# A delta-rule attention with a routed MoE behind it: first expert in parts of 320 and 160 tokens, down tiles in different PSUM tensors, VectorE's substitution in the third pair

## Chip, core and metric

One core of one Trainium2 chip. The metric is the time of one execution in device microseconds.

## What is computed

Attention with a state per head (4 batches, 8 heads, 768 tokens, head size 48), then a mixture of 8 experts (384 to 1024 to 384) on its output. The router is sticky: a token takes its own best expert or that of the token before it.

```python
for t in range(S):                      # per batch and head, state is 48 x 48
    y[t] = q[t] @ state
    state += beta[t] * outer(k_n[t], v[t] - state.T @ k_n[t])
logits = x @ w_gate;  keep = sigmoid(x @ w_local) >= 0.5
e = prev_e if keep and prev_e >= 0 else argmax(logits)
out[t] = softmax(logits)[e] * (relu(x[t] @ w1[e]) @ w2[e])
```

With the reference's inputs the first expert gets 295 tokens of the first 512 positions and 135 of the last 256 (counted from the reference's own routing).

## The kernel before

The attention works in 12 chunks of 64 tokens, two to a pair. Tokens within a pair couple through a triangular system of 32 rows. For a pair m the kernel does, in this order:

- `K(n)` (lines 234 to 261), once per chunk: loads keys and queries into two tiles `W`, multiplies them on TensorE, and writes masked products to `gt`, `G2` and `am` (pool `amp`, 6 tiles; `am` of chunk n is held until the chunk's last product, `p2`).
- `T_(m)` (262 to 313): VectorE turns `gt` into `L` (line 269), takes norms and scales (271 to 284), and then runs the substitution, 31 steps of two instructions (lines 297 and 298; 301 and 302 in the first pair, which has 15 steps). In five pairs they are on GpSimd, with `L` and `X` in tiles of their own. In the pair marked `'D'` in `MODE` they are on VectorE, `L` and `X` are two tiles of the pool `W`, and the running solution is in one of the three PSUM tensors `pr`. Then VectorE transposes the solution into `TT` and `TX` (310, 313), of which there is one each.
- `Tc(n)` and `online(n)` (337 to 423): products with `TT` and `TX` into `XT`, and then the recurrence of chunk n: `R` (line 382, VectorE), `p1`, `Us` (396), `p3` and `S_` (403), `p2`, `y` (409, 410), the store of y and a transposed copy for the router's logits (412 to 422).

The MoE (`graph`, 578 to 815) routes in two stages: z=0 after the first 16 blocks of 128 tokens (chunks 0 to 7), z=1 after all 24. The first expert is computed in two parts. Part one takes up to `LOT` tokens of stage 0, part two the rest, up to 480 in all. Each part gathers its tokens (line 741, GpSimd), transposes them on TensorE (742), does 8 up groups of 9 matmuls (750, helper line 542), splits the result into two halves on ScalarE and VectorE (543, 544, 752), and does its down products in tiles of 128 tokens, 24 matmuls each (756, helper line 549), which VectorE scales (559) and GpSimd scatters (532). The second expert (791 to 812) has 496 tokens; they are gathered once the list `gi2` is there and transposed by DMA (788, 789). Its down tiles alternate between the two halves of one PSUM tensor, `Sps`. The other six experts follow in `rest` (834 to 928), in a fixed order.

Everything up to `rest` is ordered by a list scheduler in the kernel (`Sched`, 42 to 145): at each time it issues the available operation of the highest rank on a free engine, on costs of its own. `RANK` adds a bias to the rank of each kind of operation and chunk, `PACE` is the distance it wants between the `p1` of two chunks, `boost` raises single operations (12e4 for what prepares the pair marked 'D'). Tiles of a pool are handed out in the order in which the program asks for them, except `pr`.

Of the kernel before, what the change touches and what calls it, by code (L numbers as in the profile page):

```python
# [33 lines left out]
def ca(n): return 200+.84*n  # L34
# [113 lines left out]
class Attn:  # L148
# [3 lines left out]
    NKV=3; NW=14; NAMP=6; NG2=6; NXT=3; NLX=2; NUS=2; PACE=11107.4; MODE=((16,'G'),(32,'G'),(32,'G'),(32,'D'),(32,'G'),(32,'G'))  # L152
    RANK={'':{-1: 91.5, 0: -760.0},
# [287 lines left out]
class Moe:  # L441
    CAPS=(480,496,480,448,416,384,384,384)
    SP=16; LOT=256; BOOST=(38e3,40e3)
# [134 lines left out]
    def graph(s,S,A):  # L578
# [13 lines left out]
        tq=[K([128,2,24],F32,"tq%d"%z) for z in range(3)]; rhs_=K([128,NS,2,5],F16,"rhs")  # L592
# [3 lines left out]
        def ob(i): return obs(i,i+1)[:,0]  # L596
        s.obf=ob
        W0=s.W0
        OH=[]
        for z,(lo,hi) in enumerate(((0,SP),(SP,NS))):  # L600
# [39 lines left out]
            if z==0:  # L640
# [27 lines left out]
                L0=(A.W(),A.W(),A.W())  # L668
# [20 lines left out]
            a0=2*z  # L689
            add(lambda sl=sl,n=n,a0=a0:V.tensor_tensor(s.oa[:,sl,a0:a0+2],s.ib[:,a0:a0+2].unsqueeze(1).to_broadcast([128,n,2]),s.ri[:,2,sl].unsqueeze(2).to_broadcast([128,n,2]),op=ALU.is_equal),r=["ri"+Z],w=["oa"+Z])  # L690
# [21 lines left out]
            for part,(c0,c1,vk) in enumerate(((0,3,[]),(3,5,["va0"]+(["va1"] if z else [])))):  # L712
                nv=c1-c0; q=A.pt()
                o=rhs_[:,:,:,c0:c1]
                for (x0,x1) in ([(0,SP)] if z==0 else [(0,SP),(SP,NS)]):
                    add(lambda x0=x0,x1=x1,c0=c0,c1=c1,a0=a0,nv=nv:V.tensor_tensor(rhs_[:,x0:x1,:,c0:c1],s.oa[:,x0:x1,a0:a0+2].unsqueeze(3).to_broadcast([128,x1-x0,2,nv]),s.vals[:,x0:x1,c0:c1].unsqueeze(2).to_broadcast([128,x1-x0,2,nv]),op=ALU.mult),r=(["oa0"] if z==0 else ["oa2"] if x0==0 else ["oa1"])+(vk[:1] if x0==0 else vk[1:]),w=[("rhs",part,x0)])
                def fq(q=q,r0=r0,r1=r1,c0=c0,c1=c1,nv=nv):
                    for i in range(r0,r1): nc.tensor.matmul(q.t[:,0:2*nv].rearrange("p (a c) -> p a c",a=2),ob(i),rhs_[:,i,:,c0:c1],start=(i==r0),stop=(i==r1-1))
                add(fq,r=obk+[("rhs",part,x) for x in ((0,) if z==0 else (0,SP))],w=[q],claim=[OB,OB2],e='P',c=50*(r1-r0)); S.ops[-1].q=r1-r0
                def fin(q=q,part=part,a0=a0,z=z,nv=nv,hi=hi):  # L720
                    t=q.t[:,0:2*nv].rearrange("p (a c) -> p a c",a=2); u=tq[z]
# [16 lines left out]
            hh=L0[1:] if z==0 else (A.W(),A.W()); hv=lambda a,f,hh=hh,N=N:f16(hh[a].t)[:,N*f:N*f+N]  # L738
            for j in range(2):
                m=min(128,N-128*j); hl=A.hz() if z==0 else A.Us(); a=a0+j; p=A.pt()  # L740
                add(lambda hl=hl,a=a,m=m,hi=hi:s.gather(f16(hl.t)[:,0:768],s.gi[:,a:a+1],m,128*hi),r=["gi"+Z]+xk,w=[hl],claim=[xT,*hh] if z==0 else [],e='I',c=1536*128)
                add(lambda p=p,hl=hl,m=m:s.xtr(p.t,f16(hl.t),m),r=[hl,CK],w=[p],e='P',c=450); S.ops[-1].q=6
                def fe(e,p=p,m=m,j=j,xv=xv):
                    i_=f16(p.t)[:,0:768].rearrange("p (a b) -> p a b",a=6)[:,:,0:m]; o=xv()[:,:,128*j:128*j+m]
                    (e.copy if e is nc.scalar else e.tensor_copy)(o,i_)
                add(fe,r=[p],p=[xT],e='AV',c=dict(A=ca(6*m),V=cv(6*m)))
            for f in range(8):
                p=A.pt(); t=A.ft(); ps=lambda p=p,N=N:p.t[:,0:N]
                add(lambda ps=ps,xv=xv,f=f:s.upm(ps(),xv(),[w.t for w in W0[:3]],f),r=[xT]+W0[:3]+[(w,'lo') for w in W0[:3]],w=[p],claim=[t,*hh],e='P',c=9*(N/2.35+4)); S.ops[-1].pc=(1.95*S.ops[-1].c['P'],S.ops[-1].c['P'],9e-3*N*1.13,9)
                add(lambda ps=ps,hv=hv,f=f:s.uphi(hv(0,f),ps()),r=[p],w=[("h"+Z,0,f)],claim=[hh[0]],e='A',c=ca(N))  # L750
                add(lambda ps=ps,t=t,N=N:s.upt(t.t[:,0:N],ps()),r=[p],w=[t],c=cv(N)+30)
                add(lambda e,t=t,hv=hv,f=f,N=N:e.tensor_tensor(hv(1,f),t.t[:,0:N],hv(0,f),op=ALU.subtract),r=[t,("h"+Z,0,f)],w=[("h"+Z,1,f)],claim=[hh[0],hh[1]],e='VG',c=dict(V=cv(N),G=cg(N)))
            for j in range(2):
# [50 lines left out]
        for j in range(nj):  # L804
            m=min(128,N-128*j); po=A.po(); a=4+j
# [28 lines left out]
    def rest(s,A):  # L834
# [69 lines left out]
        for e in range(2,E):  # L904
# [97 lines left out]
```

## Time and profile before

| | us |
|---|---|
| median of 3 runs | 525.1 |
| the three runs | 515.48, 525.1, 525.91 |
| profiled execution | 522.56 |
| its span, first to last instruction | 520.8 |
| mean granted TensorE clock | 0.842 |

1.8 us of the profiled execution lie outside its span. TensorE (PE) is busy 77% of the span, VectorE (DVE) 66%, GpSimd (POOL) 44%, ScalarE (ACT) 36%; the chain that ended last, as the page gives it, is only the last store, so the order of the stages has to be read from their own windows.

### The profile page before, as it was taken

What the parts mean: (1) busy time and instruction counts of PE and PEld (TensorE: products, weight loads), DVE (VectorE), ACT (ScalarE), POOL (GpSimd) and SP (SyncE); (2) the same over time, 40 slices, a digit from 0 to 9 for tenths busy, and PEclk for the clock granted to TensorE, in tenths of its full rate; (3) what the DMA queues carried; (4) which work ended last, traced back from release to release, by engine and by line L of the source; (5) the groups of instructions that cost most, each with busy time, mean ns of one, the idle gap of its engine ahead of it and who ended that gap; (6) DMA issues with size and microseconds to landing.
All of it is one profiled execution on the core that took longest, in us unless ns stands there. A gap on an engine that the chain in (4) does not pass through costs nothing. (4 is left out here: it accounts for less than half of the span.)

```text
span 520.8 us, 19200 instructions
## 1 busy us (share of the span) xinstructions
PE 400.9 (77%) x8423; PEld 299.3 (57%) x8423; DVE 341.5 (66%) x738; ACT 186.5 (36%) x330; POOL 229.8 (44%) x411
## 2 busy tenths in 40 slices
PE   4526768556577784967885898889999997999991
PEld 3515767555566684856763753455645555555661
DVE  4899136977884783694676539338586975868540
ACT  5322344332736436426520215115052341515110
POOL 5488888840189789812004412141341414041211
PEclk9775576677788867585897699999999999999997
DMA  8920053343358476147631393264837666575100
GB/s 330 395 111 5 6 125 90 108 135 136 73 184 235 117 186 184 55 113 193 126 105 57 85 228 118 82 203 126 223 112 180 188 167 188 138 238 146 46 17 27
DMA packets 63479, 72.65 MB, mean 139 GB/s; under 512 B 41972, under 2 KB 53296, under 8 KB 63393
## 3 DMA queue, kind: packets, MB, share of 16 engines
q1 hardware_dynamic: 59840, 61.34, 41.0%
q0 software_dynamic: 3552, 10.06, 6.5%
q8 instruction: 67, 1.10, 0.9%
q14 instruction: 20, 0.16, 0.1%
HBM read 52.63 MB, written 10.05 MB: 120 GB/s over the span
## 5 line engine op out<-in xcount | busy, mean ns | idle before, releaser
L297 POOL TENSOR_TENSOR fg<-L,X 128x31 f32<-128x31 f32 (+15 forms) x124 | 65.3, 527 | 40.1 <-DVE X L282 30.6
L298 POOL TENSOR_TENSOR X<-X,fg 128x31 f32<-128x31 f32 (+15 forms) x124 | 74.3, 599 | 9.7
L549 PEld LDWEIGHTS <-W 128*128 128x128 f16 (+2 forms) x492 | 49.5, 101 | 35.7 <-issue 5.1
L543 ACT ACTIVATE W<-pr 128x384 f16<-128x384 f32 (+6 forms) x56 | 26.7, 481 | 113.8 <-PE pr L542 102.2
L544 DVE TENSOR_SCALAR gf<-pr 128x384 f32<-128x384 f32 (+6 forms) x72 | 40.0, 556 | 23.8 <-ACT W L543 10.7
L542 PE MATMUL pr<-kv,W 128*128 128x384 f16 (+3 forms) x192 | 50.4, 343 | 3.9 <-DVE tx L827 2.2
L212 PE MATMUL pr<-W 64*64 64x128 f32 x768 | 33.0, 327 | 26.0 <-DMA W<-in_kq_dram 12.2
L212 PE MATMUL pr<-S,W 64*64 64x48 f32 x1408 | 35.6, 265 | 20.2 <-issue 4.3
L212 PEld LDWEIGHTS pr<-S,W 64*64 64x64 f32 x1408 | 32.6, 180 | 23.0 <-issue 4.6
L212 PEld LDWEIGHTS pr<-W 64*64 64x64 f32 x768 | 28.3, 167 | 28.3 <-issue 10.4
L542 PEld LDWEIGHTS <-W 128*128 128x128 f16 x336 | 33.5, 101 | 18.2 <-issue 1.0
L532 POOL DMA_INDIRECT out_dram<-y,so x9 | 11.2, 1239 | 53.4 <-DVE y L559 51.0
L212 PE MATMUL pr<-R,xtp 64*64 64x48 f32 x704 | 32.4, 264 | 1.1 <-issue 1.1
L530 POOL DMA_INDIRECT G<-xs,gi x25 | 26.2, 1046 | 14.9 <-DVE pvs L832 7.0
L212 PEld LDWEIGHTS pr<-R,xtp 64*64 64x64 f32 x704 | 31.3, 182 | 1.3 <-issue 1.2
L542 PE MATMUL pr<-kv,amp 128*128 128x448 f16 (+2 forms) x120 | 31.0, 351 | 0.6 <-issue 0.4
L549 PE MATMUL Sps<-W,W 128*128 128x384 f16 (+2 forms) x126 | 24.5, 326 | 4.2 <-DVE kf L559 4.2
L542 PE MATMUL pr<-kv,xtp 128*128 128x496 f16 (+2 forms) x72 | 25.5, 355 | 0.0
L527 DVE SCALAR_TENSOR_TENSOR W<-W,W 128x768 f16<-128x768 f32 (+1 forms) x17 | 19.6, 1154 | 8.1 <-ACT W L525 8.0
L259 DVE TENSOR_TENSOR amp<-pr,mask 128x512 f32<-128x512 f32 x24 | 16.4, 684 | 12.8 <-ACT gt L256 5.7
L410 DVE SCALAR_TENSOR_TENSOR y<-pr,y 128x768 f16<-128x768 f32 x12 | 11.4, 952 | 20.4 <-ACT y L409 20.4
L532 POOL DMA_INDIRECT out_dram<-S,so x8 | 11.2, 1404 | 30.4 <-DVE S L559 27.7
(357 smaller groups left out, 932.2 us busy)
## 6 DMA issues: line engine op xcount, KB each, us to landing
W<-in_kq_dram SPq DMA_DIRECT2D x24, 512.0 KB
W<-in_moe_w_dram SPq DMA_DIRECT2D x25, 384.0 KB
kv<-in_kv_dram SPq DMA_DIRECT2D x12, 768.0 KB
W<-in_moe_w_dram SPq DMA_DIRECT2D x18, 512.0 KB
xs<-y SPq DMA_DIRECT2D x12, 384.0 KB
amp<-in_moe_w_dram SPq DMA_DIRECT2D x6, 512.0 KB
amp<-in_moe_w_dram SPq DMA_DIRECT2D x6, 384.0 KB
G<-xs,gi POOLq DMA_INDIRECT x25
```

Source lines behind the costliest of these rows:

```text
L212: mm=lambda o,l,r,st,sp,tp:MM(o,l,r,start=st,stop=sp,skip_group_check=True,tile_position=tp)
L259: add(lambda n4=n4,gv=gv:nc.vector.tensor_tensor(n4(am.t),gv()[:,:,:,64:128],s.mask.unsqueeze(1).unsqueeze(1).to_broadcast([128,2,4,64]),o ...
L297: eng.tensor_tensor(tv,l[:,j,j+1:].unsqueeze(2).to_broadcast([128,n,k]),x[:,j,0:k].unsqueeze(1).to_broadcast([128,n,k]),op=ALU.mult)
L298: eng.tensor_tensor(x[:,j+1:,0:k],x[:,j+1:,0:k],tv,op=ALU.subtract)
L410: add(lambda:nc.vector.scalar_tensor_tensor(y.t[:,:,1,:],py.t[:,:,0:384],256.0,y.t[:,:,0,:],op0=ALU.mult,op1=ALU.subtract),r=[py,(y,0)],w= ...
L527: def wlo(s,st,w,k): s.nc.vector.scalar_tensor_tensor(s.wv(w,k)[:,1],s.wst(st,k),256.0,s.wv(w,k)[:,0],op0=ALU.mult,op1=ALU.subtract)
L530: return s.nc.gpsimd.indirect_dma_start(out=x[0:m],out_offset=None,in_=s.xs[0:nt,:],in_offset=bass.IndirectOffsetOnAxis(ap=ix[0:m],axis=0) ...
L532: I=s.nc.gpsimd.indirect_dma_start(out=s.out[:,:],out_offset=bass.IndirectOffsetOnAxis(ap=ix[0:m],axis=0),in_=y[0:m],in_offset=None,bounds ...
L542: for k in range(3): s.nc.tensor.matmul(ps,s.wv(W[k],k)[:,a,0,128*f:128*f+128],xT[:,3*b+k,:],start=(x==0 and k==0),stop=(x==2 and k==2))
L543: def uphi(s,h,ps): s.nc.scalar.activation(h,ps,AF.Relu,scale=2.0**-6)
L544: def upt(s,t,ps): s.nc.vector.tensor_scalar(t,ps,0.0,2.0**-6,op0=ALU.max,op1=ALU.mult)
L549: s.nc.tensor.matmul(po[0:m],h(a,f)[:,c:c+m],s.wv(W[k],k)[:,b,f%2,:],start=(x==0 and f==0),stop=(x==2 and f==7))
```

## The change

- `MODE`: the pair on VectorE is the third and not the fourth. GpSimd then solves pairs one, two, four, five and six.
- `LOT`: part one of the first expert takes 320 tokens and not 256, in down tiles of 128, 128 and 64; part two takes 160 and not 224, in tiles of 64 and 96. A tile of 64 uses `downc` (48 matmuls on half of the array's columns, two side by side) and `yoc` (two scalings and a copy of the weights). Part one holds five tiles `W` and not three, and there is one gather and one scatter more. The indices and weights of the 64-token tile of part two are copied to partitions 0 to 63 (`gb`, `sb`, `pvb`), four small VectorE instructions more.
- Down tiles of the second expert alternate between a half of `pr` and a half of `Sps`; those of part two do so as well.
- `RANK` and `PACE` (11107.4 to 18432.4) have other numbers throughout.

```diff
-    ...PACE=11107.4; MODE=((16,'G'),(32,'G'),(32,'G'),(32,'D'),(32,'G'),(32,'G'))
+    ...PACE=18432.4; MODE=((16,'G'),(32,'G'),(32,'D'),(32,'G'),(32,'G'),(32,'G'))
...
-    SP=16; LOT=256; BOOST=(38e3,40e3)
+    SP=16; LOT=320; BOOST=(38e3,40e3)
...
-                L0=(A.W(),A.W(),A.W())
+                L0=tuple(A.W() for _ in range(5))
...
+                        if z: V.tensor_scalar(gb[0:64],u[64:128,0:1,4],float(96*128),float(128*hi-1),op0=ALU.add,op1=ALU.min)
...
+                        x=0 if z==0 else 64; V.tensor_tensor(pvb[z][0:64],u[x:x+64,2-2*z:3-2*z,8],u[x:x+64,2-2*z:3-2*z,9],op=ALU.add)
...
+                    if z: V.scalar_tensor_tensor(sb[0:64],u[64:128,0:1,5],float(96*32),u[64:128,0:1,2],op0=ALU.add,op1=ALU.add)
...
-                m=min(128,N-128*j); po=A.pt() if z==0 else A.po(); y=A.kf(); a=a0+j
+                po=A.pt() if z==0 or j else A.po(); y=A.kf(); k=2 if m==64 else 1
...
+                    dn=lambda ...:(s.downm if k==1 else s.downc)(po.t[:,0:384],hv,[None]*3+[w.t for w in W0[3:]],(f,f+1),c0,m)
...
-            m=min(128,N-128*j); po=A.po(); a=4+j
+            m=min(128,N-128*j); po=A.po() if j%2 else A.pt(); a=4+j
```

## Rows read from the trace of the kernel before

**Rows 1.** Stretches: start:end, length, busy PE, PEld, DVE, ACT, POOL, clock, DMA, GB/s.

```profile
111.80:140.80 29.00, 19.02 (x728) 17.51 (x727) 22.10 (x50) 12.61 (x25) 0.00 (x0) 0.74 0.43 113
...
281.00:291.00 10.00, 3.32 (x61) 3.08 (x62) 5.86 (x26) 1.44 (x2) 3.01 (x3) 0.50 0.23 75
...
305.40:345.70 40.30, 34.72 (x187) 19.24 (x188) 20.93 (x30) 10.45 (x15) 7.11 (x6) 1.00 0.45 136
345.70:511.70 166.00, 158.17 (x1105) 92.45 (x1103) 115.73 (x200) 54.20 (x83) 45.90 (x39) 1.00 0.53 149
```

**Rows 2.** GpSimd in time order, 73 to 224 us: start, duration, instruction, idle before.

```profile
73.12 0.24 POOL L297 TENSOR_TENSOR fg<-L,X 128x31 f32<-128x31 f32 x1
...
140.84 0.24 POOL L297 TENSOR_TENSOR fg<-L,X 128x31 f32<-128x31 f32 x1 [29.13 <-DVE X L282]
...
181.45 1.04 POOL L297 TENSOR_TENSOR fg<-L,X 128x31 f32<-128x31 f32 x1 [1.42 <-DVE X L282]
...
223.49 0.25 POOL L298 TENSOR_TENSOR X<-X,fg 128x31 f32<-128x31 f32 x1
```

**Rows 3.** VectorE in time order, 70 to 259 us.

```profile
70.53 0.96 DVE L410 SCALAR_TENSOR_TENSOR y<-pr,y 128x768 f16<-128x768 f32 x1 [11.92 <-ACT y L409]
...
96.01 0.95 DVE L382 TENSOR_TENSOR R<-kv,pr 128x768 f32<-128x768 f32 x1
...
97.10 1.75 DVE L283 TENSOR_TENSOR W<-W,mm 128x512 f32<-128x512 f32 x2
...
116.32 0.94 DVE L382 TENSOR_TENSOR R<-kv,pr 128x768 f32<-128x768 f32 x1
...
141.18 0.95 DVE L382 TENSOR_TENSOR R<-kv,pr 128x768 f32<-128x768 f32 x1 [0.51 <-PE pr L212]
...
149.35 0.20 DVE L298 TENSOR_TENSOR pr<-pr,fv 128x31 f32<-128x31 f32 x1
...
155.02 0.94 DVE L382 TENSOR_TENSOR R<-kv,pr 128x768 f32<-128x768 f32 x1
...
229.35 2.28 DVE L313 STREAM_TRANSPOSE TX<-X 128x256 f32<-128x256 f32 x4
...
242.74 0.95 DVE L382 TENSOR_TENSOR R<-kv,pr 128x768 f32<-128x768 f32 x1
...
258.13 0.96 DVE L527 SCALAR_TENSOR_TENSOR amp<-W,amp 128x768 f16<-128x768 f32 x1 [0.73 <-ACT amp L525]
```

**Rows 4.** TensorE in time order, 76 to 88 us: chunk 1's products, then K(7).

```profile
78.59 3.63 PE L212 MATMUL pr<-R,xtp 64*64 64x48 f32 x64
...
84.44 1.92 PE L212 MATMUL pr<-Us,amp 64*64 64x48 f32 x64
86.15 2.09 PE L212 MATMUL pr<-W 64*64 64x128 f32 x64
```

**Rows 5.** Busy time of line 527 alone (weight casts) in GpSimd's last pair.

```profile
180.10:223.80 43.70, 7.07 (x6) 0.69 0.49 139
```

**Rows 6.** TensorE in time order, 281 to 316 us.

```profile
285.61 0.82 PE L538 MATMUL pr<-mident,Us 128*128 128x128 f16 x6 [4.76 <-DMA Us<-xs,gi]
...
298.13 1.89 PE L542 MATMUL pr<-xtp,W 128*128 128x224 f16 x18
305.38 0.37 PE L542 MATMUL pr<-kv,W 128*128 128x496 f16 x1 [0.21 <-DMA kv<-G]
311.03 1.14 PE L549 MATMUL Sps<-amp,W 128*96 128x384 f16 x6
```

**Rows 7.** What TensorE waited for, 305.4 to 345.7 us: total, times, longest.

```profile
PE Sps L549 <- DVE kf L559: 4.9, 5, 1.4
```

**Rows 8.** TensorE in a 64-token down tile of a later expert: first and last rows.

```profile
403.30 0.36 PE L554 MATMUL Sps<-amp,W 128*64 128x192 f16 x4
...
405.22 0.25 PE L554 MATMUL Sps<-X,W 128*64 128x192 f16 x2
```

**Rows 9.** ScalarE's last cast of the third expert's weights before its start at 345.66.

```profile
329.40 0.84 ACT L525 ACTIVATE xtp<-amp 128x768 f16<-128x768 f32 x1 [0.58 <-DMA amp<-in_moe_w_dram]
```

More of the change, by code (lines that the diff above doesn't have):

```diff
@@ L148 @@
 class Attn:
-    NKV=3; NW=14; NAMP=6; NG2=6; NXT=3; NLX=2; NUS=2; PACE=11107.4; MODE=((16,'G'),(32,'G'),(32,'G'),(32,'D'),(32,'G'),(32,'G'))
-    RANK={'':{-1: 91.5, 0: -760.0},
[17 rows of a table removed]
+    NKV=3; NW=14; NAMP=6; NG2=6; NXT=3; NLX=2; NUS=2; PACE=18432.4; MODE=((16,'G'),(32,'G'),(32,'D'),(32,'G'),(32,'G'),(32,'G'))
+    RANK={'':{0: -3.1},
[17 rows of a table added]
     def __init__(s, ctx, tc, kq,kv,beta,xs,wg,wl,lg,cap):
@@ L549, in downm, with downc @@
                 s.nc.tensor.matmul(po[0:m],h(a,f)[:,c:c+m],s.wv(W[k],k)[:,b,f%2,:],start=(x==0 and f==0),stop=(x==2 and f==7))
-    def downc(s,po,h,W,c,m):
+    def downc(s,po,h,W,fs,c,m):
         k=128//m; w=384//k
-        for f in range(8):
+        for f in fs:
             for x,(a,b) in enumerate(((0,0),(0,1),(1,0))):
@@ L591, in graph @@
         b5=K([128,E],F32,"b5"); tl=K([128,E],F16,"tl"); c8=K([128,E,E],F32,"c8"); pE=K([128,E,E],F32,"pE"); key=K([128,E],F32,"key")
-        tq=[K([128,2,24],F32,"tq%d"%z) for z in range(3)]; rhs_=K([128,NS,2,5],F16,"rhs")
+        tq=[K([128,3,10] if z==0 else [128,2,10] if z==1 else [128,2,24],F32,"tq%d"%z) for z in range(3)]; gb,sb=K([128,1],I32,"gib"),K([128,1],I32,"sob"); pvb=[K([128,1],F32,"pvb%d"%z) for z in range(2)]; FQ0=[]; rhs_=K([128,NS,2,5],F16,"rhs")
         scs=[[K([128,2,32] if i==2 else [128,32],F32,"sc%d"%i) for i in range(4)]]*2
@@ L713, in graph, with fq, fin @@
                 nv=c1-c0; q=A.pt()
-                o=rhs_[:,:,:,c0:c1]
+                rv=lambda z=z:rhs_.rearrange('p i a c -> p (i a c)').rearrange('p (i a c) -> p i a c',a=3-z,c=5)
                 for (x0,x1) in ([(0,SP)] if z==0 else [(0,SP),(SP,NS)]):
[L716 to L721, printed above, removed]
+                    add(lambda x0=x0,x1=x1,c0=c0,c1=c1,a0=a0,nv=nv,na=na,rv=rv:V.tensor_tensor(rv()[:,x0:x1,:,c0:c1],s.oa[:,x0:x1,a0:a0+na].unsqueeze(3).to_broadcast([128,x1-x0,na,nv]),s.vals[:,x0:x1,c0:c1].unsqueeze(2).to_broadcast([128,x1-x0,na,nv]),op=ALU.mult),r=(["oa0"] if z==0 else ["oa2"] if x0==0 else ["oa1"])+(vk[:1] if x0==0 else vk[1:]),w=[("rhs",part,x0)]); S.ops[-1].pre.update(FQ0 if z else ())
+                def fq(q=q,r0=r0,r1=r1,c0=c0,c1=c1,nv=nv,na=na,rv=rv):
+                    for i in range(r0,r1): nc.tensor.matmul(q.t[:,0:na*nv].rearrange("p (a c) -> p a c",a=na),ob(i),rv()[:,i,:,c0:c1],start=(i==r0),stop=(i==r1-1))
+                add(fq,r=obk+[("rhs",part,x) for x in ((0,) if z==0 else (0,SP))],w=[q],claim=[OB,OB2],e='P',c=50*(r1-r0)); S.ops[-1].q=r1-r0; FQ0+=[S.ops[-1]] if z==0 else []
+                def fin(q=q,part=part,a0=a0,z=z,nv=nv,hi=hi,na=na):
+                    t=q.t[:,0:na*nv].rearrange("p (a c) -> p a c",a=na); u=tq[z]
                     if part==0:
@@ L737, in graph, with fe @@
             xT=L0[0] if z==0 else A.W(); xv=lambda xT=xT,N=N:f16(xT.t)[:,0:6*N].rearrange("p (a b) -> p a b",a=6)
[L738 to L741, printed above, removed]
+            hh=L0[1:] if z==0 else (A.W(),A.W()); per=8//(len(hh)//2); hv=lambda a,f,hh=hh,N=N,per=per:f16(hh[len(hh)//2*a+f//per].t)[:,N*(f%per):N*(f%per)+N]
+            col=lambda t,a:(lambda:t[:,a:a+1])
+            TL=[(128,col(s.gi,0),col(s.so,0),col(s.pv,0)),(128,col(s.gi,1),col(s.so,1),col(s.pv,1)),(64,col(s.gi,2),col(s.so,2),col(pvb[0],0))] if z==0 else [(64,col(gb,0),col(sb,0),col(pvb[1],0)),(N-64,col(s.gi,3),col(s.so,3),col(s.pv,3))]
+            c0=0
+            for m,g_,_,_ in TL:
+                hl=A.hz() if z==0 else A.Us(); p=A.pt()
+                add(lambda hl=hl,g_=g_,m=m,hi=hi:s.gather(f16(hl.t)[:,0:768],g_(),m,128*hi),r=["gi"+Z]+xk,w=[hl],claim=[xT,*hh] if z==0 else [],e='I',c=1536*m)
                 add(lambda p=p,hl=hl,m=m:s.xtr(p.t,f16(hl.t),m),r=[hl,CK],w=[p],e='P',c=450); S.ops[-1].q=6
-                def fe(e,p=p,m=m,j=j,xv=xv):
-                    i_=f16(p.t)[:,0:768].rearrange("p (a b) -> p a b",a=6)[:,:,0:m]; o=xv()[:,:,128*j:128*j+m]
+                def fe(e,p=p,m=m,c0=c0,xv=xv):
+                    i_=f16(p.t)[:,0:768].rearrange("p (a b) -> p a b",a=6)[:,:,0:m]; o=xv()[:,:,c0:c0+m]
                     (e.copy if e is nc.scalar else e.tensor_copy)(o,i_)
-                add(fe,r=[p],p=[xT],e='AV',c=dict(A=ca(6*m),V=cv(6*m)))
+                add(fe,r=[p],p=[xT],e='AV',c=dict(A=ca(6*m),V=cv(6*m))); c0+=m
             for f in range(8):
@@ L753, in graph @@
-            for j in range(2):
-                m=min(128,N-128*j); po=A.pt() if z==0 else A.po(); y=A.kf(); a=a0+j
+                add(lambda e,t=t,hv=hv,f=f,N=N:e.tensor_tensor(hv(1,f),t.t[:,0:N],hv(0,f),op=ALU.subtract),r=[t,("h"+Z,0,f)],w=[("h"+Z,1,f)],claim=list(hh),e='VG',c=dict(V=cv(N),G=cg(N)))
+            c0=0
+            for j,(m,_,o_,v_) in enumerate(TL):
+                po=A.pt() if z==0 or j else A.po(); y=A.kf(); k=2 if m==64 else 1
                 for f in range(0,8,2):
-                    add(lambda po=po,hv=hv,f=f,j=j,m=m:s.downm(po.t[:,0:384],hv,[None]*3+[w.t for w in W0[3:]],(f,f+1),128*j,m),r=[("h"+Z,b,g) for b in range(2) for g in (range(8) if z==0 else (f,f+1))]+W0[3:]+[(w,'lo') for w in W0[3:]],w=[po],claim=list(hh),e='P',c=6*168); S.ops[-1].pc=(1.95*S.ops[-1].c['P'],S.ops[-1].c['P'],2.6,6)
-                add(lambda y=y,po=po,a=a,m=m:s.yo(f32(y.t)[:,0:384],po.t[:,0:384],s.pv[:,a:a+1],m),r=[po,"pv"+Z],w=[y],c=cv(384)+40)
-                add(lambda y=y,a=a,m=m:s.scatter(f32(y.t)[:,0:384],s.so[:,a:a+1],m),r=[y,"so"+Z],e='I',c=1536*128)
+                    dn=lambda po=po,hv=hv,f=f,c0=c0,m=m,k=k:(s.downm if k==1 else s.downc)(po.t[:,0:384],hv,[None]*3+[w.t for w in W0[3:]],(f,f+1),c0,m)
+                    add(dn,r=[("h"+Z,b,g) for b in range(2) for g in (range(8) if z==0 else (f,f+1))]+W0[3:]+[(w,'lo') for w in W0[3:]],w=[po],claim=list(hh),e='P',c=6*168/k); S.ops[-1].pc=(1.95*S.ops[-1].c['P'],S.ops[-1].c['P'],2.6,6*k)
+                add(lambda y=y,po=po,v_=v_,m=m,k=k:(s.yo if k==1 else s.yoc)(f32(y.t)[:,0:384],po.t[:,0:384],v_(),m),r=[po,"pv"+Z],w=[y],c=(cv(384)+40)*(1+.3*(k-1)))
+                add(lambda y=y,o_=o_,m=m:s.scatter(f32(y.t)[:,0:384],o_(),m),r=[y,"so"+Z],e='I',c=1536*m); c0+=m
@@ L916, in rest @@
                 m=min(128,n-128*j); po=pso()[:,0:384]; y=s.f32(yo())[:,0:384]; a=4*e+j
-                if m in (32,64): s.downc(po,lambda z,f:h(z,f,n),W[e],128*j,m); s.yoc(y,po,s.pv[:,a:a+1],m)
+                if m in (32,64): s.downc(po,lambda z,f:h(z,f,n),W[e],range(8),128*j,m); s.yoc(y,po,s.pv[:,a:a+1],m)
                 else: s.downm(po,lambda z,f:h(z,f,n),W[e],range(8),128*j,m); s.yo(y,po,s.pv[:,a:a+1],m)
```

15 lines of the change are left out of this document (7 added, 8 removed), and 34 rows, old and new, of the table RANK.

## The prediction

> **What bounds the kernel now.** The page's chain holds only the last store, so I first cut the span by what each engine does and read busy time by stretch [rows 1]. Behind 345.7 us TensorE is busy 158.2 of 166.0 us at the full clock: six experts, untouched by the change, which only moves their start. From 305.4 to 345.7 it is busy 34.7 of 40.3. In front of that no engine is full, so there the order of dependences counts, and for that I took GpSimd alone, in time order [rows 2]: it solves pair after pair, the third from 73.12 to 111.7; then it stands for 29.13 us, and goes on 140.84 to 180.0 and 181.45 to 223.7. In the hole it waits for VectorE's last preparation of the fifth pair, not for work of its own; the fourth pair is meanwhile on VectorE, from line 283's end at 98.85 to 149.55 [rows 3]. The chunks of the last pair can't begin before 223.7: chunk 10's R follows at 242.74 [rows 3]. From there to the second expert's start at 305.38 there is one chain: two chunks, the router's second stage, the gathers and DMA transposes. At that start TensorE has waited 0.21 us for tokens [rows 6], so in 291 to 305 part two of the first expert and the arrival of those tokens are in balance.
>
> **Part 1, the substitution on the third pair.** Removed from GpSimd: pair three, 73.12 to 111.7. Added to it: pair four. The number of solves is the same, and what counts is where the hole goes. GpSimd is free at 73.1 as before, and then needs pair four's L. In the kernel before this was ready when line 283 had ended, 97.10 + 1.75 = 98.85 [rows 3]. What comes in front is not the substitution: K(7) needs the am tile that chunk 1 gives back with its p2, and the p2 row ends at 86.36, beside K(7)'s start at 86.15 (the next instruction overlaps the end of the one before) [rows 4]. I keep 98.9 as the start of pair four on GpSimd. Bounds: earlier by 7, if TensorE's p1 of chunk 1 (78.59, [rows 4]) comes as soon as chunk 0 is done with its y (70.53 + 0.96 = 71.5, [rows 3]); later by 11, if the substitution, now beside chunks 0 and 1, does to them what it did to chunks 2 to 4. That price is in the rows of R [rows 3]: with a PSUM tensor and VectorE shared, and some work queued between, chunk 4 followed chunk 3 after 141.18 - 116.32 = 24.9 us, and without, chunk 5 followed chunk 4 after 13.8, so 11.1 us more.
>
> From 98.9 nothing should stop GpSimd: pair five needs p2 of chunk 3, and pair six that of chunk 5, whose pair (the third) VectorE can finish early. VectorE has time for it while GpSimd solves pair two: the row at 70.53 shows 11.92 us of idle time ahead of it [rows 3]. Its work is 62 instructions, which fill at most the 50.7 us from 98.85 to 149.55, with much else between them. Three solves last 38.6 (73.12 to 111.7), 39.2 and 42.3 us [rows 2], and I allow 0.7 us for each of two seams (0.1 and 1.4 in the rows). End: 98.9 + 38.6 + 39.2 + 42.3 + 1.4 = 220.4, against 223.7: **-3.3 us**.
>
> What is late next is the way from there to chunk 10's R, 19.0 us. Of it 5.6 us (223.74 to 229.35, [rows 3]) are spent because VectorE is in the router's first stage when pair six ends. That stage waits for chunk 7, whose pair would now end near 137 and not at 149.5, so it can be over in time; but VectorE does something else in such places too. Between 0 and 5.6 I take about the middle: **-3.0 us**.
>
> The weight casts of line 527 are tied to buffers and not to pairs; they take 7.07 us in the last pair [rows 5], which is the longest by 3 to 4 us. The Trainium skill, page "SBUF — State Buffer", section "Who interferes with whom", says that a VectorE instruction with both inputs in SBUF and a GpSimd instruction that reads SBUF shut each other out for their whole length. That is one reading of the longer pair, and it speaks against packing the solves without a hole; the price of this is the second rival below.
>
> **Part 2, 320 and 160 tokens.** TensorE's steps at full clock: 18 up matmuls of 224 tokens take 1.89 us, 6 down matmuls 1.14 [rows 6]; without the last one's latency that is some 0.094 us for 224 columns and 0.163 for 384. The difference, 0.069 for 160 columns, makes 0.027 for 64. Part one: 72 x 0.027 = +1.9. Its third tile is 48 half-wide matmuls: those of a later expert went from 403.30 to 405.47 [rows 8], +2.2. So +4.1 us; its two full tiles stay as they are. Part two: -1.9 for the ups, and tiles of 64 and 96 cost 2.2 + 3.9 and not 7.8: -3.6 us in all. The Trainium skill, page "TensorEngine Tiling (Array Packing)", section "Restrictions", says that column tiling switches Fast Weight Load off, which speaks against such tiles; here 48 loads with their matmuls fit into those 2.2 us against 3.9 us for a full tile. By the rule, with no gain from packing, each such tile would be 3.9, and the sum 1.7 us worse for part one and for part two.
>
> Where does it land? The +4.1 I cost at nothing: TensorE is idle 6.7 of the 10 us from 281 to 291 [rows 1], 4.76 of them in one wait for part two's tokens [rows 6]; without that cover it is +4.1. Part two's -3.6 is no gain ahead of 305.38, where the tokens of the second expert decide. But 18 of part two's down matmuls stand behind that start (6 at 311.03 [rows 6], and 12 more by form), 18 x 0.163 = 2.9 us on an engine that is the limit there: **-2.9 us**. The router's chain gets four more VectorE instructions of 0.17 us, **+0.7**. One more gather and one more scatter (1.0 to 1.5 us on GpSimd) come after its solves, where it is nearly empty. The two more tiles W delay loads of the second expert's weights; VectorE's last cast of them ended at 259.1 [rows 3], 46 us before their use, which hides it.
>
> **Part 3, PSUM tensors.** TensorE waits five times, 4.9 us in all, until VectorE has read the other half of Sps [rows 7]. In the alternation no two tiles next to each other share a tensor, so the waits go, on an engine that is the limit. What is late next: the third expert's weights, whose last cast ends at 330.24 [rows 9] (VectorE's half 1 us later), 14.4 us before use. **-4.9 us**; bound 0, if the shared pr tensors make a like wait.
>
> **New ranks.** Each list of biases is bound to its own order and can't be priced by rows. It is why the bounds above are wide.
>
> **Sum.** Against the profiled execution: 522.6 - 3.3 - 3.0 - 2.9 + 0.7 - 4.9 = 509.2, **509 us**. That execution lies 0.5% below the median of the three runs. About 2%, 10.5 us, is what a measurement of this kernel can tell from no change.
>
> **Rivals.**
> 1. *The first expert's gain is hidden.* Part one's extra 4.1 us stand ahead of the router's matmuls and push the tokens of the second expert, and the shorter part two only makes TensorE wait for them. Then parts 2 and 3 give 4.1 + 0.7 - 4.9, about 0, and the attention -6.3: 516. For it: the 0.21 us. Against it: 6.7 us of idle time at 281 to 291.
> 2. *The solves run slower without the hole.* The hole of 29 us gave VectorE 22.1 us of work without GpSimd beside it [rows 1]. If that now meets the solves and all three last 42.3 us, they end at 98.9 + 126.9 + 1.4 = 227.2: +3.5, with no gain behind it, and -7.1 from the rest: 519. That is what the rule of the Trainium skill's page "SBUF — State Buffer" would make of it. Against it: the third pair's solve had VectorE's substitution beside its last 13 us and was the shortest of the three (38.6).
> 3. *Slower.* The substitution holds one of three PSUM tensors while chunks 0 and 1 need two, and K(6) and K(7) one each. If K(7) slips by both distances that were long in the kernel before (24.9, and 116.32 - 96.01 = 20.3 from chunk 2 to 3, against 13.8: 17.6 us; [rows 3]), pair four starts at 116.5 and the solves end at 238.0: +14.3. With -4.9 + 0.7 of the rest and no gain in the last chunks, 533. It turns slower than before from a start of pair four at about 112. For it: the PSUM hold of 50 us in the kernel before. Against it: VectorE's idle 11.92 us ahead of 70.53, which would shorten that hold.
> 4. *It doesn't do what it says*: more than 320 or 160 tokens for the parts, and a pass of the overflow loop. The reference's routing gives 295 and 135, so this falls out.
>
> **How the numbers follow.** Forecast 0.50 (498 to 516), rival 1 0.18, rival 2 0.17, rival 3 0.15. The forecast's lower end: pair four 7 us earlier, the whole 5.6 us, 509.2 - 7 - 2.6 = 499.6, and 1.5 more for the last solve without casts. The range is 498 to 525; the upper end takes in rivals 1 and 2 and leaves out most of rival 3 and a small part below. Faster by over 2% is below 514.6: most of the forecast and a few of the rivals' lower parts, 0.47. Slower by over 2% is above 535.6: under half of rival 3 and what I have not seen, 0.09. The rest, 0.44, is within 2%.
>
> **What would show it.** Right: GpSimd's solve of pair four starts between 92 and 105, pairs five and six follow with under 2 us between, the last ends at 209 to 224; VectorE's substitution lies before 90; the up matmuls of 160 tokens end before the second expert's first matmul, and the row "Sps waits for kf" is gone, with that expert's stretch near 33 us. Wrong: a start of pair four past 110, holes between solves, a longer way than 63 us from chunk 10's R to the second expert, or a hole ahead of its start.

## The result and the profile after

The changed kernel takes 516.5 us (median of 20; before, beside it, 522.7): a ratio of 0.987, 95% interval 0.984 to 0.990. Its profiled execution spans 512.5 us, before's 520.8. Forecast was 509, which is 0.974. Some executions of any kernel take some per cent longer, so the ratios here and below count only those within 1.5% of their kernel's fastest. Stage by stage, from marks on the timelines (in the kernel after, lines behind 750 stand 8 lower); each column is one execution, and executions of the same program differ by up to 6 us at one of these marks:

| mark, us | before | after | difference |
|---|---|---|---|
| GpSimd's last solve ends | 223.7 | 215.8 | -8.0 |
| R of chunk 10 | 242.7 | 235.7 | -7.0 |
| R of chunk 11 | 256.5 | 249.6 | -6.9 |
| last logits (line 422) | 270.5 | 268.0 | -2.5 |
| expert 2's first matmul | 305.4 | 301.4 | -4.0 |
| expert 3's first matmul | 345.7 | 335.7 | -9.9 |
| end | 520.8 | 512.5 | -8.3 |

GpSimd in time order, after; it answers to [rows 2]. The hole now stands ahead of pair four, and the seams are 0.1 us:

```profile
73.15 0.26 POOL L298 TENSOR_TENSOR X<-X,fg 128x31 f32<-128x31 f32 x1
94.91 0.51 POOL L297 TENSOR_TENSOR fg<-L,X 128x31 f32<-128x31 f32 x1 [21.50 <-DVE X L282]
...
133.32 0.58 POOL L298 TENSOR_TENSOR X<-X,fg 128x31 f32<-128x31 f32 x1
133.98 0.24 POOL L297 TENSOR_TENSOR fg<-L,X 128x31 f32<-128x31 f32 x1
...
174.07 0.25 POOL L298 TENSOR_TENSOR X<-X,fg 128x31 f32<-128x31 f32 x1
174.40 0.24 POOL L297 TENSOR_TENSOR fg<-L,X 128x31 f32<-128x31 f32 x1
...
214.99 0.79 POOL L298 TENSOR_TENSOR X<-X,fg 128x31 f32<-128x31 f32 x1
```

Between R of chunk 11 and the last logits 4.4 of the 6.9 us are lost again. First the window of that stretch in the kernel before (its length, busy time and instructions of PE, PEld, DVE, ACT and POOL, then PEclk, DMA share and GB/s), and TensorE's costliest group in it (busy time, mean ns, idle before it):

```profile
256.50:270.50 14.00, 13.10 (x287) 11.45 (x288) 9.58 (x23) 5.42 (x11) 0.00 (x0) 1.00 0.59 119
```

```profile
L542 PE MATMUL pr<-W,W 128*128 128x256 f16 x63 | 7.3, 273 | 0.0
```

The same two of the kernel after, and three lines of TensorE's timeline there:

```profile
249.60:268.00 18.40, 17.20 (x297) 12.42 (x296) 11.49 (x24) 6.46 (x12) 0.00 (x0) 0.96 0.45 114
```

```profile
L542 PE MATMUL pr<-W,W 128*128 128x320 f16 x71 | 11.4, 316 | 0.9 <-DVE y L410 0.9
```

```profile
251.31 1.15 PE L212 MATMUL pr<-S,W 64*64 64x48 f32 x64
252.43 1.38 PE L542 MATMUL pr<-W,W 128*128 128x320 f16 x9
253.75 2.07 PE L212 MATMUL pr<-R,xtp 64*64 64x48 f32 x64
```

TensorE is nearly full there in both kernels. Its up matmuls of part one, queued between the steps of chunk 11 (one group of 1.38 us stands between its state product and its triangular product) and ahead of its logits, take 4.1 us more. Seven groups stand there in both kernels: they take 9.2 us instead of 7.3. The other 2.2 us are an eighth group, which in the kernel before runs ahead of chunk 11's R. About 1 us of the added 4.4 is the lower clock (0.96): in e2 and e5 below, where the program is the same up to there, the stretch takes 17.1 and 17.3 us.

The second gain is expert 2's own stretch, 34.4 us after 40.3. TensorE's waits after 300 us, kernel after (us in total, times, longest): the five waits of [rows 7] for kf (VectorE's scaled copy of a finished down tile) are gone. Here tx is a copy of token positions, and gf a copy of an up group.

```profile
PE pr L542 <- DVE tx L835: 3.3, 3, 2.4
PE pr L542 <- DMA kv<-G: 3.2, 1, 3.2
PE pr L542 <- DVE gf L544: 2.7, 7, 0.7
```

### The profile page after: what moved, and what is told of

Read it like the earlier page. It is cut to its first block, busy times and chain, and to the rows that moved or that the text cites. A ratio compares the mean times of both kernels' runs of the same rounds, so it can differ in the third digit from the quotient of the medians.

```text
span 512.5 us, 19383 instructions
## 1 busy us (share of the span) xinstructions
PE 402.6 (79%) x8501; PEld 296.4 (58%) x8501; DVE 345.0 (67%) x746; ACT 186.9 (36%) x331; POOL 233.1 (45%) x414
## 5 line engine op out<-in xcount | busy, mean ns | idle before, releaser
L298 POOL TENSOR_TENSOR X<-X,fg 128x31 f32<-128x31 f32 (+15 forms) x124 | 73.4, 592 | 9.7
L542 PE MATMUL pr<-kv,amp 128*128 128x384 f16 (+4 forms) x240 | 66.5, 357 | 7.4 <-DMA kv<-G 3.2
L549 PEld LDWEIGHTS <-W 128*128 128x128 f16 (+2 forms) x512 | 51.2, 100 | 32.5 <-issue 0.5
L543 ACT ACTIVATE W<-pr 128x384 f16<-128x384 f32 (+5 forms) x52 | 26.7, 513 | 93.5 <-PE pr L542 65.0
L542 PEld LDWEIGHTS <-amp 128*128 128x128 f16 x240 | 24.0, 101 | 29.4 <-issue 11.0
L542 PEld LDWEIGHTS <-W 128*128 128x128 f16 x240 | 22.7, 103 | 13.9 <-issue 2.3
L542 PE MATMUL pr<-kv,W 128*128 128x384 f16 (+2 forms) x96 | 30.1, 355 | 0.0
L212 PE MATMUL pr<-R,xtp 64*64 64x48 f32 x704 | 28.4, 245 | 0.3 <-DVE R L382 0.2
L212 PEld LDWEIGHTS pr<-R,xtp 64*64 64x64 f32 x704 | 27.2, 163 | 0.8 <-issue 0.5
L527 DVE SCALAR_TENSOR_TENSOR amp<-W,amp 128x768 f16<-128x768 f32 (+1 forms) x20 | 22.5, 1131 | 4.5 <-ACT amp L525 4.5
L543 ACT ACTIVATE xtp<-pr 128x160 f16<-128x160 f32 (+3 forms) x20 | 8.7, 437 | 45.3 <-PE pr L542 44.6
```

The lines of the kernel that those rows point to most:

```text
L212: mm=lambda o,l,r,st,sp,tp:MM(o,l,r,start=st,stop=sp,skip_group_check=True,tile_position=tp)
L298: eng.tensor_tensor(x[:,j+1:,0:k],x[:,j+1:,0:k],tv,op=ALU.subtract)
L527: def wlo(s,st,w,k): s.nc.vector.scalar_tensor_tensor(s.wv(w,k)[:,1],s.wst(st,k),256.0,s.wv(w,k)[:,0],op0=ALU.mult,op1=ALU.subtract)
L542: for k in range(3): s.nc.tensor.matmul(ps,s.wv(W[k],k)[:,a,0,128*f:128*f+128],xT[:,3*b+k,:],start=(x==0 and k==0),stop=(x==2 and k==2))
L543: def uphi(s,h,ps): s.nc.scalar.activation(h,ps,AF.Relu,scale=2.0**-6)
L549: s.nc.tensor.matmul(po[0:m],h(a,f)[:,c:c+m],s.wv(W[k],k)[:,b,f%2,:],start=(x==0 and f==0),stop=(x==2 and f==7))
```

## Experiments

All are compared with runs of before on the same chip. Stages in us, from each profiled execution; "solves" is their end, "stretch" lies between the first matmuls of experts 2 and 3. The profiled execution of e10 lay 1.4% above its median, so its stages are left out of the table.

```
run                              solves  logits  logits-E2  stretch  E3-end  logits-end   ratio [95%]
before                            223.7   270.5     34.8      40.3    175.1     250.3
after                             215.8   268.0     33.4      34.4    176.8     244.5     0.987 [0.984, 0.990]
e1  expert 2's tensors alone      220.8   267.6     34.3      42.0    174.3     250.6     0.999 [0.994, 1.005]
e2  expert 2's tensors undone     217.4   264.8     35.3      36.0    176.7     248.0     0.991 [0.986, 0.996]
e3  pair and ranks alone          219.7   269.3     34.5      41.5    174.9     250.9     1.000 [0.995, 1.005]
e4  pair alone                    229.0   275.5     36.4      44.6    174.6     255.6     1.029 [1.017, 1.040]
e5  part two's tile undone        220.7   270.7     35.6      37.8    176.6     250.0     1.006 [1.002, 1.011]
e6  all tensors, rest of before   220.8   264.9     37.3      37.1    178.5     252.8     1.014 [1.011, 1.018]
e7  transposes later              216.6   265.8     53.2      40.0    175.8     269.0     1.039 [1.032, 1.046]
e8  transposes and ups later      221.2   270.1     53.4      40.8    177.1     271.3     1.044 [1.033, 1.056]
e9  pair and ranks undone         221.6   271.4     37.9      40.6    176.3     254.8     1.025 [1.020, 1.031]
e10 all tensors undone               -       -         -         -        -         -     0.999 [0.996, 1.003]
e11 ups in steps, later           220.4   263.7     42.8      35.0    175.0     252.8     1.000 [0.996, 1.003]
e12 ranks undone                  230.6   275.4     39.9      41.4    179.2     260.5     1.017 [1.012, 1.023]
```

**e1 and e2: expert 2's four down tiles.** The edit is put into the kernel before, and taken out of the kernel after:

```diff
-            m=min(128,N-128*j); po=A.po(); a=4+j
+            m=min(128,N-128*j); po=A.po() if j%2 else A.pt(); a=4+j
```

> The kernel before with one edit: expert 2's down tiles alternate between Sps and a free tensor; ranks, modes and the first expert's parts stay. Theory (the five waits for kf are the whole worth of this part): the stretch from expert 2's first up matmul to expert 3's, 40.28 us before, shrinks by 4 to 5 us to about 35.5, the waits of Sps for kf of 4.9 us go, and the time falls by 4 to 5 us (ratio about 0.991). Rival (the stretch of the changed kernel is shorter because part two's leftover downs moved ahead of expert 2): the stretch stays at 39.5 us or more and the time within 1 us.

> The changed kernel with expert 2's four down tiles all in Sps again; nothing else differs, and the program is the same up to expert 2's stretch. Theory (the waits are the worth): the stretch, 34.35 us in the changed kernel, grows to 38.5 to 39.5, with four or five waits of Sps for kf, and the time is 4 to 5 us longer than the changed kernel's, about 521 us on the scale of a kernel before of 522.7 (ratio to before about 0.996). Rival (leftover downs moved ahead are the worth): the stretch stays under 36 us and the ratio stays at about 0.987.

The theory fell in e1, and e2 came nearer to its rival. TensorE's waits after 300 us in e1:

```profile
PE pr L542 <- DVE gf L544: 3.9, 8, 1.3
PE pr L542 <- DVE tx L827: 3.3, 3, 2.4
PE Sps L549 <- DVE kf L559: 1.4, 2, 0.7
PE pr L549 <- DVE gf L544: 1.4, 1, 1.4
```

The waits for kf fell from 4.9 to 1.4 us, but a down tile in pr now waited 1.4 us for the up groups that use pr, the longest wait of an up group for its pr half rose from 0.7 to 1.3 us, and the time stayed. Not all of the long stretch of 42.0 us is waiting: TensorE's idle time there fell from 5.6 to 4.5 us, but this execution had 0.92 of the clock in it. In the changed kernel the alternation is worth 36.0 - 34.4 = 1.6 us of stretch, which the times can't tell from nothing (the two intervals overlap); the rest of the 5.9 us is there without it. The Trainium skill, page "Perfetto Trace Analysis", section "Optimizing Tensor Performance", asks for independent matmul groups to rotate through PSUM banks so that evictions overlap; e1 shows a case in which that gains nothing: 3.5 us of waits go, new ones come in pr, and the ratio is 0.999.

**e3 and e4: the pair, with and without the new ranks**, in the kernel before:

```diff
-MODE=((16,'G'),(32,'G'),(32,'G'),(32,'D'),(32,'G'),(32,'G'))
+MODE=((16,'G'),(32,'G'),(32,'D'),(32,'G'),(32,'G'),(32,'G'))
```

e3 has PACE and RANK of the kernel after too.

> The kernel before with the third pair on VectorE and the changed kernel's ranks and pace; first expert in 256 and 224 and expert 2's tiles in Sps as before. Theory (the third gather and the longer up groups of the first expert take back what the solves gain): the last pair ends on POOL near 216 as in the changed kernel, chunk 10's R is at 236 or earlier, the router's second stage starts 6 to 7 us ahead of before's 270.75, at about 264, and the ratio is about 0.988. Rival (the tail between R and the router loses its 4.5 us for another reason, such as the order by the new ranks): the second stage starts at 267 to 269 as in the changed kernel, and the ratio is 0.995 to 1.0.

> The kernel before with one edit, the third pair on VectorE instead of the fourth; before's ranks and pace. Theory (the place of the substitution alone brings pair four's start forward, since GpSimd's pairs need then only the preparation of pair four by VectorE): pair four starts on GpSimd at 92 to 105 us and the last pair ends at 212 to 221 us, against 223.74 before. Rival (the ranks bring it): pair four starts after 105 us, behind VectorE's substitution of pair three, and the last pair ends at 222 us or later; the ratio is then 1.0 or above.

Pair four starts at 97.4 and at 103.2 us, so the place alone brings it forward, but with before's ranks it comes later and the time is 2.9% longer. The output product of chunk 1, from which pair four's preparation follows, runs at 88.3 us in e4 and at 75.8 in the changed kernel; ahead of it TensorE waits 4.3 us for VectorE to read a pr tensor. It is near to what the third rival feared, a PSUM tensor held while VectorE substitutes. With the new ranks the solves end 4.0 us earlier and the time doesn't move: R of chunk 10 gains only 1.1 us. It comes 21.9 us after the solves' end, where three executions of before's program up to there took 19.0, 18.0 and 17.2. The stretch from R of chunk 11 to the logits is 13.0 us here, so the theory's part on the longer up groups stands, but not its price: without them the gain is lost one step earlier.

**e5 and e6: the second tile of part two.** e5 undoes this move alone in the kernel after:

```diff
-                po=A.pt() if z==0 or j else A.po(); y=A.kf(); k=2 if m==64 else 1
+                po=A.pt() if z==0 else A.po(); y=A.kf(); k=2 if m==64 else 1
```

e6 makes both moves of tensors in the kernel before.

> The changed kernel with one edit: the second tile of part two of the first expert (96 tokens) is summed in Sps again instead of in a tile of pr; expert 2's tiles still alternate. Theory A (the stretch of expert 2 became short because part two's tile left Sps, whose two halves expert 2's tiles then found free): the stretch grows from 34.35 us to 38 us or more with waits of Sps for kf of 2 us or more, and the ratio to before rises from 0.987 to 0.993 or above. Theory B (it became short because a part two of 160 tokens needs less work behind expert 2's start: 36 matmuls of 0.163 us of downs fewer are left over): the stretch stays at 34.4 to 35.5 us and the ratio at 0.985 to 0.990.

> The kernel before with both moves of tensors (part two's second tile in pr, expert 2's tiles in turn in pr and Sps), and the first expert still in 256 and 224, the fourth pair on VectorE, before's ranks. Theory A (tensors): the stretch of expert 2, 40.28 us before, falls to 36 us, and the ratio to before is 0.99 or lower. Theory B (size of part two): part two's left-over downs of about 2.9 us stay inside the stretch and the ups wait for tiles of pr, so the stretch is 39 us or more and the ratio 0.995 to 1.005.

e5 goes for theory A: stretch 37.8, 2.0 us of waits of Sps for kf, ratio 1.006. But e6 has theory A's short stretch (37.1, with TensorE idle for 2.4 us of it instead of 5.6) and theory B's ratio or worse. Its profiled execution was 1.1% faster than its median, so its stages don't carry the whole ratio; what they show is that the gain is given back ahead of expert 2 (37.3 us instead of 34.8) and behind expert 3's start (3.4 us). Ahead of expert 2 it goes in one place:

```profile
297.78 3.40 PE L542 MATMUL pr<-xtp,W 128*128 128x224 f16 x18 [2.11 <-DVE gf L544]
```

TensorE waits there for VectorE's copy of an up group, and the matmuls behind the wait take 3.4 us at 0.58 of the clock, 1.9 at full clock.

**e7 and e8: what stands in the way of chunks 10 and 11.** A gate only orders the planner's queue:

```diff
# e7: the token transposes of part one
+S.ops[-1].gate=[A.chx[10]['fk']] if z==0 else []
# e8: also its up groups
+S.ops[-1].gate=[A.chx[11]['p2']] if z==0 else []
```

> The changed kernel with the planner holding the first expert's three token transposes back until chunk 10's first state product is issued on TensorE; the same operations otherwise. Theory (the two waits of TensorE for gathers, 3.34 and 3.33 us, stand in chunk 10's way and take back part of what the solves gain): R of chunk 10 comes 4 to 6 us earlier than 235.7 us, at 230 to 232, the last logits 3 to 5 us earlier than 268.0, and the ratio to before falls to 0.977 to 0.981. Rival (chunk 10 waits for something else at that time, so the waits for gathers cost nothing): R of chunk 10 stays at 234 us or later and the ratio at 0.985 or above.

> As the run before, and part one's up groups are held back as well until chunk 11's last output product is issued. Theory (up groups of 1.4 us and more between R of chunk 11 and the last logits take back 4.5 us of the attention part's gain): the last logits come 10.5 to 14 us after R of chunk 11, against 18.4 us in the changed kernel and 14.1 us before, expert 2 starts 5 us or more ahead of 301.4 us, and the ratio to before is 0.970 to 0.978. Rival (expert 2's start is bound by TensorE's work of part one and two, so what moves behind the logits is added there): the logits come earlier, but expert 2 starts at 299 us or later, and the ratio is that of the run with the transposes alone or above.

Both rivals were nearer, and the price was far larger. R of chunk 10 comes 16.7 us after the solves in e7, and 16.6 in e2, which has the waits for gathers. But that same program also took 18.7 (e5), 19.9 (the changed kernel) and 21.3 us (e10), so what the waits cost chunk 10, if anything, is below what one execution shows. In e8 the way from chunk 11's R to the logits still takes 16.9 us, with the up groups held back: the theory named 10.5 to 14. And TensorE's timeline of e7 shows expert 2's positions behind all of part two:

```profile
302.64 0.56 PE L831 MATMUL pr<-R,gt 128*128 128x20 f16 x16
...
319.01 0.57 PE L542 MATMUL pr<-kv,amp 128*128 128x496 f16 x1 [14.25 <-DMA kv<-G]
```

In the changed kernel that product runs at 284.4. The planner ranks the first expert above it, so held-back work comes out ahead of it.

**e9 and e10: the rest of the change without the pair and its ranks, and without the tensors.** e9 is the kernel after with before's MODE, PACE and RANK; e10 undoes the edits of e2 and e5 together.

> The changed kernel with the attention part's settings of before: the fourth pair on VectorE again, with before's ranks and pace; first expert in 320 and 160 and the moved tensors stay. Theory (the pair's move gives nothing at the last logits, and all of the gain lies behind them, in parts and tensors together): from the last logits to the end 244 to 247 us, as in the changed kernel (244.5), and the ratio to before is 0.985 to 0.991. Rival (the pair's move carries 3 to 4 us of the gain, the amount by which the last pair ends earlier at like clock): the ratio is 0.993 to 0.998.

> The changed kernel with both moves of tensors undone: part two's second tile and all of expert 2's in Sps. Theory (parts and tensors pay only together): logits to end 250 us or more against 244.5 us in the changed kernel and 250.3 us before, and the ratio to before 0.998 to 1.010. Rival (the parts alone carry it, and the run with part two's tile in Sps was slow because the alternation met that tile): logits to end 246 to 248 us and the ratio 0.988 to 0.994.

e9 met neither theory: 2.5% slower, with 254.8 us from logits to end. In its profile 18 down matmuls of part one, behind a wait of 3.1 us, take 5.6 us at 0.52 to 0.63 of the clock, 2.9 at full clock. e10 bears out the theory by its time. The changed kernel, e2, e5 and e10 share ranks and parts, and their programs are the same up to some 311 us, so here the order of the queue is no rival to the tensors:

| part two's tile | expert 2's tiles alternate | all in Sps |
|---|---|---|
| moved | 0.987 | 0.991 |
| in Sps | 1.006 | 0.999 |

The gain hangs on part two's tile; the alternation adds at most a little to it, and nothing without it. In this program the parts without the tensors give nothing, and with before's ranks neither tensors (e6) nor parts and tensors (e9) gain. New ranks, pair and tensors with before's parts were not run, so it is not shown that the parts are needed.

**e11: part one's up groups in steps.** The gate of e8 in a milder form; part two's up groups are gated too, behind the product for expert 2's positions, which the expectation below leaves out:

```diff
+S.ops[-1].gate=[A.chx[11]['p1']]*(f>0)+[A.chx[11]['p2']]*(f>2)+[A.chx[11]['lf']]*(f>4) if z==0 else []
```

> The changed kernel with the planner holding part one's up groups back in steps: the first as it is, the next two behind chunk 11's triangular product, two more behind its output product, the last three behind its logits; part two's transposes and everything else as planned. Theory (the up groups of 320 columns between R of chunk 11 and the last logits, where the changed kernel takes 18.4 us and before 14.1 us, take back the solves' gain): that stretch falls to 13.5 to 15.5 us, expert 2 starts 1.5 to 4 us earlier against the last logits' own shift of 3 to 4 us, and the ratio to before is 0.977 to 0.983. Rival (the work moved behind the logits delays expert 2's positions by as much): the stretch falls, logits to end grows from 244.5 us to 247 us or more, and the ratio stays at 0.985 to 0.990.

From R of chunk 11 to the logits 13.5 us: with the up groups out of the way the stretch is as short as before's, though TensorE now waits 1.6 us of it for the transfer of xt. But the rival holds for the time. Windows of e11 up to and behind the logits, to the product for expert 2's positions:

```profile
250.20:263.70 13.50, 11.87 (x263) 9.00 (x262) 8.71 (x18) 5.26 (x9) 0.00 (x0) 0.95 0.61 156
263.70:291.60 27.90, 23.21 (x200) 13.04 (x197) 17.50 (x68) 2.21 (x5) 5.03 (x8) 0.69 0.03 10
```

and the second stretch in the changed kernel, where it is 16.4 us:

```profile
268.00:284.40 16.40, 12.89 (x166) 9.34 (x164) 14.91 (x61) 0.73 (x2) 5.81 (x9) 0.90 0.12 40
```

Work that leaves the one queue place stands in the next, here also at a lower clock (0.69 against 0.90).

**e12: before's ranks and pace in the kernel after.**

> The changed kernel with only the ranks and the pace of before: third pair on VectorE, first expert in 320 and 160, moved tensors. Theory (the order that the ranks give is worth as much as all three parts, since each part alone left the time where it was or made it longer): pair four starts on GpSimd at 100 us or later, logits to end is 250 us or more against 244.5 us in the changed kernel, and the ratio to before is 1.010 to 1.035. Rival (the ranks only hold pair four's preparation, and what lies behind the logits follows from parts and tensors): pair four starts at 100 us or later, but logits to end stays at 244 to 248 us, and the ratio is 0.990 to 1.003.

The theory holds: 1.017 instead of 0.987, pair four at 105.7, 260.5 us from logits to end. Of the five kernels that have before's ranks and something of the change (e1, e4, e6, e9, e12), four are slower than before by 1.4% or more. These ranks were fitted to another program, so e12 gives the price of a wrong fit and not what the new ranks add to a right one. None of the runs is faster than the changed kernel.

## Why the prediction was right in its sign and range, and wrong in its terms

The gain is half of what was forecast, and under the 2% that a measurement was said to tell.

- *Solves, -3.3.* Right, though the profile shows -8.0. Kernels whose program is the same up to that point differ by how late chunk 1's output product comes (below): before's program ends its solves at 220.8 to 221.6 (e1, e6, e9) or 223.7, where that product takes 1.92 us and e1's 1.11; the changed one at 215.8 to 218.0 (after, e2, e7, e10) or 220.4 to 221.2 (e5, e8, e11). Like with like that is some -2.5 to -5.8. Pair four's start at 94.9 lies in the forecast's 92 to 105. Not right: VectorE's substitution was not over before 90, but ran from 50.2 to 100.5; pair four's preparation came in between, and so its length didn't matter.
- *The way to chunk 10's R, -3.0.* It isn't to be seen: 19.0 us before, 19.9 after, and 16.6 to 21.3 in other executions of the changed program up to there. VectorE is in the router's first stage again when the solves end; TX follows 5.8 us after them (before 5.6).
- *Part one's +4.1 us, cost at nothing.* One half of it was placed rightly: the third tile of down matmuls (+2.2) runs where TensorE waits for part two's tokens:

```profile
280.48 1.22 PE L554 MATMUL pr<-amp,W 128*64 128x192 f16 x12
282.72 0.35 PE L538 MATMUL pr<-mident,Us 64*128 64x64 f16 x6 [1.03 <-DMA Us<-xs,gib]
283.00 0.69 PE L554 MATMUL pr<-W,W 128*64 128x192 f16 x12
```

  The other half, the wider up matmuls (+1.9), was not: most of them lie at 250 to 268, between chunk 11's R and its logits, where TensorE had 0.9 us free in 14.0. They cost their 1.9 us there, and the eighth group that moved in with them 2.2. This is the first half of rival 1, work ahead of the router's matmuls. Its second half came too: TensorE waits 3.2 us for expert 2's tokens ahead of that expert's start (line L542 with kv<-G above; 0.2 us before). Rival 1's 516 is also the measured time, but by luck: it let parts and tensors come to nothing and the attention keep its gain, and the measured gain lies in expert 2's stretch. How much of the attention's gain is left, the profiles don't tell: the last logits come at 270.5, 267.6 and 264.9 us in three programs with before's attention part and at 268.0, 264.8 and 270.7 in three with the changed kernel's (after, e2, e5).
- *Four more VectorE instructions, +0.7.* Not to be seen: from the logits to expert 2 the changed kernel, e2 and e5 take 33.4 to 35.6 us, before and e1 34.8 and 34.3.
- *Left-over downs, -2.9.* Behind expert 2's start there are now 24 half-wide matmuls, 1.24 us, instead of 18 full ones: -1.7. Half-wide tiles cost 2.5 us for 48, a little more than the 2.2 I took and well under the 3.9 of a full tile, so the reading of the Trainium skill's page "TensorEngine Tiling (Array Packing)", section "Restrictions", by which packing would gain nothing, is not borne out here.
- *PSUM tensors, -4.9.* The bound 0 that I named, a like wait in pr, is what e1 shows. In the changed kernel TensorE's idle time in the stretch is 0.4 us; it is 2.1 without the alternation (e2) and 4.8 without part two's move (e5). With before's parts and ranks both moves take it from 5.6 to 2.4 (e6), and the time doesn't follow.
- *New ranks, not priced.* With ranks fitted to another program the kernel is 3% slower (e12), and the pair alone 2.9% (e4 beside e3), as much as the whole forecast gain. "Can't be priced by rows" was true, but the bounds should then have reached farther to the slow side.
- *Rival 2* falls: without the hole the three solves last 39.0, 40.3 and 41.4 us, 120.7 together, before 120.1. If VectorE and GpSimd shut each other out (the Trainium skill, "SBUF — State Buffer", "Who interferes with whom"), packing the solves without a hole did not make it dearer here. *Rival 3* is e4 and e12 in small: pair four at 103 to 106, and slower than before, but by the logits that is 5 us in both; the rest of it, 5 and 10 us, comes behind them.
- Of the signs named, two of "wrong" came true: 65.7 us, over 63, from chunk 10's R to expert 2, and a hole ahead of that expert's start (3.2 us).

So in the profiles the gain lies behind the logits: 250.3 us to the end before, 244.5 after, -5.8 beside -6.2 of the medians. Only the stretch's -5.9 stands clear of the spread; -1.5 ahead of it and +1.6 behind do not. Open is why the clock is low behind the waits that e6 and e9 have ahead of expert 2, and what held chunk 10's R back in e3: no run took one of these waits alone.

## What to carry to other kernels

Work that is "hidden under idle time" has to be queued in that idle time: look up the stretch where the queue will place it, and how full that is. Where an order is fitted to a whole program, parts of a change have no price of their own; undo them one at a time from the full change as well as add them one at a time, and compare stages between marks, not absolute times. One profile a kernel is little: look for runs whose program is the same up to a mark before a difference there is given a cause. A free PSUM half was no gain by itself (e1), where another rotation used it.

## What the runs showed of the hardware that was not expected

The same program differed by 3 to 4 us in one place, for two reasons. TensorE's output product of chunk 1 in the changed kernel:

```profile
75.78 1.22 PE L212 MATMUL pr<-Us,amp 64*64 64x48 f32 x64
78.00:82.00 4.00, 0.87 (x16) 0.87 (x20) 4.00 (x9) 2.30 (x5) 0.00 (x0) 0.80 0.60 242
```

and in e5, whose instructions are the same to that point:

```profile
76.46 0.44 PE L212 MATMUL pr<-Us,amp 64*64 64x48 f32 x14
78.91 1.63 PE L212 MATMUL pr<-Us,amp 64*64 64x48 f32 x50 [2.01 <-issue]
78.00:82.00 4.00, 3.09 (x82) 2.96 (x81) 3.46 (x8) 0.81 (x1) 0.00 (x0) 0.50 0.76 301
```

First, a hole of 2.0 us behind the 14th matmul, in which TensorE waits for nothing that the profile shows ("issue"). The trace has DMA packets of 16 KB on a queue that it calls instruction: in e5 one from 76.7 to 77.8 us, ahead of the hole's end by 1.1 us; in the changed kernel the like one from 73.4 to 74.7, over before the product starts. In all six runs with a hole at this matmul (e3, e5, e7, e8, e10, e11; 0.4 to 2.0 us) it ends 1.1 to 1.4 us after such a packet; in the changed kernel and e2, which have none, the packet is over before the product starts. Five more holes of 0.4 to 1.5 us in the changed kernel between 42 and 58 us, 4.4 us in sum and "issue" too, end 1.3 to 1.5 us after such packets. So TensorE most likely stands there for want of its own instructions; that the packet is TensorE's, and why it comes later, is not shown. Second, the lower level of the clock (0.50, 1.2 GHz) behind the hole: in e10, with the same hole but 0.78 of the clock from 78 to 82 us, pair four starts at 97.1, in e5 at 98.5, in the changed kernel at 94.9. That makes some 2 us for the hole and 1.4 for the clock.

In expert 6 TensorE waits 2.4 us for tx in the changed kernel and in e1. Kernel after, from that wait's end:

```profile
427.40:430.00 2.60, 2.51 (x12) 1.34 (x12) 0.61 (x6) 0.40 (x2) 1.99 (x3) 0.73 0.70 226
430.00:433.00 3.00, 3.00 (x14) 1.59 (x13) 1.24 (x3) 1.52 (x3) 0.88 (x1) 0.67 0.45 132
```

and e1, from the end of the same wait (2.39 us):

```profile
435.60:438.00 2.40, 2.39 (x15) 1.46 (x15) 0.72 (x6) 0.68 (x2) 1.79 (x2) 1.00 0.70 228
438.00:441.00 3.00, 3.00 (x21) 1.79 (x19) 2.61 (x5) 1.99 (x4) 1.00 (x1) 1.00 0.44 142
```

With the lower clock after it expert 6's stretch is 29.3 us instead of e1's 27.6, as much as the changed kernel's profiled execution loses behind expert 3's start. Why an equal wait is followed by one clock here and the other there, no run tells.
